# A decode block with attention over a cache and a gated feed-forward: the mask of the PV product pinned in DVE's order, gate and up rows loaded in three pieces, end of attention written ahead of the wd rows

## The chip, the cores and the metric

The kernel runs on one core of one Trainium2 chip. The metric is the device time of one execution in microseconds (us), the median of several runs. The engines of a core work side by side, each through its own list of instructions in order: PE (matrix multiplies; PEld is its weight load), DVE (elementwise work and reductions), ACT (activations), POOL and SP. In this kernel SP issues all large transfers from HBM, one after the other; 16 DMA engines carry them. SBUF is the on-chip memory of 128 partitions, PSUM the accumulators of PE.

## What is computed

One token goes through two branches that are added to it. All data are float32.

```python
def _A_ref(x, k_cache, v_cache, wq, wo):          # x [1,1,576]; caches [1,32,16384,128]
    q = (x @ wq).reshape(B, Sq, H, Dh).transpose(0, 2, 1, 3)
    scores = jnp.einsum("bhqd,bhkd->bhqk", q, k_cache) * (Dh ** -0.5)
    p = _softmax(scores, axis=-1)
    o = jnp.einsum("bhqk,bhkd->bhqd", p, v_cache)
    return o.transpose(0, 2, 1, 3).reshape(B, Sq, H * Dh) @ wo

def _B_ref(x, w_gate, w_up, w_down):              # 576 -> 4608 -> 576
    g = jnp.einsum("bsd,df->bsf", x, w_gate)
    u = jnp.einsum("bsd,df->bsf", x, w_up)
    return jnp.einsum("bsf,fd->bsd", _gelu(g) * u, w_down)

xn = _layernorm(x)
return x + _A_ref(xn, ...) + _B_ref(xn, ...)
```

The two caches hold 32 heads x 16384 positions x 128 numbers each, 537 MB together; the weights add 50 MB. Everything is read once.

## The kernel before

*Memory.* Three large slots of 128 partitions x 64 KiB (`slot()`) hold whatever is being streamed. A slot is handed out again when every reader of its last content has finished; the load into it waits for that on SP, and all later loads wait behind it, as SP issues in order.

*Start.* The first slot (`mix`) takes the remainders of wq, gate and up (`row3`: the fourth row of each partition, `tails`: the last 64 rows), the second wq. `project(steps, ...)` multiplies the normalised token with a weight matrix: one step for each row j of a partition, 12 matmuls a step for gate and up (two passes each in the trace, 24), all accumulating in the same PSUM tile `pg`. `ffn(which)` loads three rows j = 0, 1, 2 of gate (then of up) into a slot with one transfer, runs the steps (row 3, tail, rows 0 to 2), copies the result with ACT into a free part `gc` of the slot (L160), and spreads it by four small POOL transfers over the partitions of `gu`. `ffn_act` makes `hT = gelu(g) * u` of it on DVE; it stands ahead of the first head's work on DVE.

*Heads.* For each of the 32 heads, K and V are loaded into one slot each (8.39 MB per transfer). `qk(h, i)` handles one of eight blocks of 16 keys per partition: DVE multiplies the block in place with the query (L196), then sums ten of the 16 keys (L200), ACT the other six (L199). `softmax(h)` finds the maximum (DVE L204, PE transpose L206, DVE L208, PE L210) and exponentiates on ACT (L214). `pv(h)` multiplies the probabilities with V on PE: 32 matmuls of 4 probability columns x 512 (L220, 64 passes), into `PO[h % 2]`, one of two PSUM tiles. Only a diagonal of each product is wanted: `out_a(h)` masks the tile with `sel` on DVE (L225, "the mask") and sums (L227), `out_b(h)` sums over partitions on PE (L231), and ACT stores the head's column (L232).

*Order.* The framework's scheduler orders the instructions of each engine; it may move an instruction away from its place in the text. `out_a(h - 1)` and `out_b(h - 1)` are written behind block i = 3 of head h. In the built order of this kernel the mask stands right behind `softmax(h - 1)` on DVE, ahead of the first multiply of head h.

*End.* The rows of wd and wo go into the three slots (two and five transfers); wd0 takes a slot that PV of head 30 frees, wd1 and the first 20 rows of wo the slot of the last K, the rest the slot of the last V. PE adds 36 wd rows with `hT` (`add_out`, 144 passes) and 32 wo rows with `oT`, the normalised attention output that comes through a transpose (L286), an ACT copy (L288) and a small transfer. Behind row 26 of wo (`MERGE`) the four partial sums are joined.

Of the kernel before, what the change touches and what calls it, by code (L numbers as in the profile page):

```python
# [13 lines left out]
P = 128  # L14
H, SK, DH = 32, 16384, 128
D, DF = 576, 4608
# [5 lines left out]
DJ = 4  # L22
# [15 lines left out]
def kernel(ctx: ExitStack, tc: tile.TileContext, x, k_cache, v_cache, wq, wo, wg, wu, wd, out):  # L38
    nc = tc.nc
# [12 lines left out]
    wmain = {n: w[:DM].rearrange("(p j) f -> p (j f)", j=DJ) for n, w in (("q", wq), ("g", wg), ("u", wu))}  # L52
# [4 lines left out]
    def slot():  # L57
        return slots.tile([P, R * DH], F32, tag="s", name="slot")

    def load(dst, src):  # L60
        nc.sync.dma_start(dst, src)
        return dst
# [4 lines left out]
    def part_of_mix(src):  # L67
        nonlocal at
        n = src.shape[1]
        at += n  # L70
        return load(mix[:, at - n : at], src)

    ROW3 = 3 * DF
    tails = {"q": part_of_mix(wtail["q"])}
    load(wq_t, wmain["q"])
    row3 = {}
# [15 lines left out]
    sel = cpool.tile([P, 4], F32, name="sel")  # L92
# [28 lines left out]
    def project(steps, group, size):  # L121
        pg = ps_big.tile([P, 3, 512], F32, tag="pb", name="pg")
        for k, (j, rhs) in enumerate(steps):
            for b in range(group // size):
                for q in range(4):
                    lo = q * group + b * size
                    if j < DJ:
                        lhs = xnb[:, j, :]
                    else:
                        lhs = xtb[:, q // 2, :]  # L130
                        lo = (q % 2) * group + b * size
                    nc.tensor.matmul(pg[32 * q : 32 * q + 32, b, :size], lhs, rhs[:, lo : lo + size],  # L132
                                     start=k == 0, stop=k == len(steps) - 1)
        return pg[:, : group // size, :size]

    steps = [(DJ, tails["q"])] + [(j, wq_t[:, j * HD : (j + 1) * HD]) for j in range(DJ)]
# [16 lines left out]
    def ffn(which):  # L153
        n = "gu"[which]
        t = slot()
        w = load(t[:, :ROW3], wmain[n][:, :ROW3])
        gc = t[:, ROW3 : ROW3 + FG]
        steps = [(3, row3[n]), (DJ, tails[n])] + [(j, w[:, j * DF : (j + 1) * DF]) for j in range(3)]
        pg = project(steps, FG, FB)
        nc.scalar.activation(gc.rearrange("p (b f) -> p b f", f=FB), pg, AF.Copy)  # L160
        for q in range(4):
            nc.gpsimd.dma_start(gu[32 * q : 32 * q + 32, which, :], gc[32 * q : 32 * q + 1, :])

    ffn(0)
    ffn(1)

    hT = cpool.tile([P, WD_T], F32, name="hT")
# [54 lines left out]

    def out_a(h):
        o4 = PO[h % 2].rearrange("p (r d) -> p r d", d=DH)
        nc.vector.tensor_mul(o4, o4, sel.unsqueeze(2).to_broadcast([P, 4, DH]))  # L225
        OM[h] = spool.tile([P, DH], F32, name="om")
        nc.vector.tensor_reduce(OM[h], o4.rearrange("p r d -> p d r"), axis=AX.X, op=ALU.add)  # L227

    def out_b(h):
        pc = ps_s.tile([P, 512], F32, tag="sm", name="pc")  # L230
        nc.tensor.matmul(pc[:, :1], OM.pop(h), ones[:, :1], start=True, stop=True)  # L231
        nc.scalar.activation(oall[:, h : h + 1], pc[:, :1], AF.Copy)  # L232

    q_spread(0)
    for h in range(H):
        KT[h] = load(slot(), kv[h])
        VT[h] = load(slot(), vv[h])
        for i in range(NSUB):
            qk(h, i)
            if h == 0 and i == 3:  # L240
                ffn_act()
            if h > 0 and i == 3:
                out_a(h - 1)
                out_b(h - 1)
        KT.pop(h)
        softmax(h)
        if h + 1 < H:
            q_spread(h + 1)
        pv(h)
# [3 lines left out]
    def add_out(pair, lhs, w, last=False):  # L253
        for i in range(2):
            q = 32 * (2 * pair + i)
            nc.tensor.matmul(acc[q : q + 1, :HALF], lhs, w[:, i * HALF : (i + 1) * HALF],  # L256
                             start=q not in seen, stop=last)
            seen.add(q)
# [7 lines left out]
    lo = n0  # L266
# [3 lines left out]
    wd_rows = [wd0[:, j * D : (j + 1) * D] for j in range(a)] + [wd1[:, j * D : (j + 1) * D] for j in range(b)]  # L270
    wo_rows = [wd1[:, (b + j) * D : (b + j + 1) * D] for j in range(n0)]
    wo_rows += [wo1[:, j * D : (j + 1) * D] for j in range(WO_T - n0)]

    out_a(H - 1)
    out_b(H - 1)
    for j, w in enumerate(wd_rows):
        add_out(j % 2, hT[:, j : j + 1], w)

    pl = ps_s.tile([P, 512], F32, tag="sm", name="pl")
    nc.tensor.matmul(pl[:, :H], ones, lsum, start=True, stop=True)  # L280
    rl = cpool.tile([P, H], F32, name="rl")
# [6 lines left out]
    nc.scalar.activation(orow, po[:H, :P], AF.Copy)  # L288
    oT = cpool.tile([P, WO_T], F32, name="oT")
    nc.gpsimd.dma_start(oT, orow)  # L290

    x2 = wo1[:, R * DH - 2 * HALF : R * DH - HALF]
    nc.vector.memset(x2, 0.0)
# [43 lines left out]
```

## Time and profile before

| | |
|---|---|
| time, median of 3 runs | 1481.46 us (1480.93 to 1481.81) |
| the profiled execution | 1480.83 us, its span 1478.9 us |
| busy: DVE / ACT / PE / PEld / POOL | 990.4 / 656.9 / 402.3 / 107.0 / 6.4 us |
| from HBM | 587.6 MB, 397 GB/s over the span |
| TensorE clock granted, mean | 0.626 |

The profile is one execution, recorded by the hardware. Its *groups* give line, engine, operation, output <- input with shapes, count, then busy time, mean ns of one instruction, and the idle time of the engine just ahead of them with what ended it. The *chain that ended last* is followed back from the last instruction, at each step to what released it. *Waits* give who waited for whom: us in total, times, longest. The *timeline* gives start, length, and the instruction. *Windows* give the busy time of each engine in a stretch, the granted clock, the mean busy share of the 16 DMA engines and what they moved; a DMA packet counts where it starts, so that in a short window the rate can be far above or below the real one. L12 is line 12 of the kernel that was profiled.

### The profile page before, as it was taken

The page shows a single profiled execution, that of the slowest core. Times are in us where ns is not written, and L with a number is a line of the kernel's source. Part 1 is how long each engine was busy: PE and PEld are TensorE (multiplying, and loading weights), DVE is VectorE, ACT ScalarE, POOL GpSimd, SP SyncE. Part 2 cuts the span into 40 slices and gives each one's busy share as a digit, 9 for nine tenths or more (in the row PEclk, how much of TensorE's full clock was granted, in tenths as well). Part 3 has the DMA queues.
Part 4 walks back from the last instruction along what each step waited for, and adds up shares of the span by engine and source line. Part 5 has one row for each costly group of instructions (what it writes and reads, how often), then busy time and mean ns, then how long its engine had stood idle before and what let it go on. Part 6 is the DMA issues. An engine that isn't in the chain of part 4 may idle for free.

```text
span 1478.9 us, 10328 instructions
## 1 busy us (share of the span) xinstructions
PE 402.3 (27%) x2881; PEld 107.0 (7%) x2881; DVE 990.4 (67%) x668; ACT 656.9 (44%) x3240; POOL 6.4 (0%) x17
## 2 busy tenths in 40 slices
PE   4413212223222112322321122232211223223118
PEld 1100000000000000000000000000000000000002
DVE  1026787676677887667678876766778776676780
ACT  0014554444445554444455544444455444444550
POOL 0000000000000000000000000000000000000000
PEclk9765555665665566566555656656555665665568
DMA  9999999999899999999989998999999999999897
GB/s 405 426 398 426 422 399 399 415 392 412 371 398 397 397 398 424 399 394 401 396 371 397 424 427 370 398 397 396 399 398 397 425 396 398 386 385 419 373 386 300
DMA packets 11791, 588.31 MB, mean 398 GB/s; under 512 B 1603, under 2 KB 1621, under 8 KB 2006
## 3 DMA queue, kind: packets, MB, share of 16 engines
q1 hardware_dynamic: 11380, 587.60, 93.4%
q8 instruction: 22, 0.36, 0.1%
q14 instruction: 35, 0.29, 0.1%
q0 software_dynamic: 352, 0.06, 0.0%
q10 hardware_dynamic: 2, 0.00, 0.0%
HBM read 587.60 MB, written 0.00 MB: 397 GB/s over the span
## 4 chain that ended last, share of the span: by engine, by line
DVE 55%; PE 24%; ACT 12%; DMA 6%; issue 3%; POOL 0%; ACTq 0%; SPq 0%; DVEq 0%
DVE slot L196 34%; PE po L220 20%; DVE s L200 18%; ACT jk L199 10%; DMA slot<-in_B_w_up_dram 3%; DMA slot<-in_A_wq_dram 2%; DVE po L225 2%; PE acc L256 1%; DMA gu<-slot 1%; PE pg L132 1%; ACT pe L214 1%; PE pb L210 1%; PE pt L206 1%; DVE pm L204 1%; DVE nm L208 1%
## 5 line engine op out<-in xcount | busy, mean ns | idle before, releaser
L199 ACT ACTIVATE jk<-slot 128x128 f32<-128x128 f32 x1536 | 475.3, 309 | 312.5 <-DVE slot L196 268.2
L196 DVE TENSOR_TENSOR slot<-slot,qs 128x2048 f32<-128x2048 f32 x256 | 573.9, 2283 | 0.0
L200 DVE TENSOR_REDUCE s<-slot 128x10 f32<-128x1280 f32 x256 | 367.6, 1478 | 0.0
L220 PE MATMUL po<-slot,pe 128*4 128x512 f32 x2048 | 289.9, 730 | 14.8 <-ACT pe L214 14.5
L199 ACT ACTIVATION_READ_ACCUMULATOR jk<-slot 128x1 f32 x1536 | 286.0, 186 | 0.0
L206 PE MATMUL pt<-ident,pm 128*1 128x128 f32 x32 | 11.9, 372 | 950.0 <-DVE pm L204 950.0
L225 DVE TENSOR_TENSOR po<-po,sel 128x512 f32<-128x512 f32 x32 | 22.4, 700 | 339.8 <-PE po L220 339.8
L232 ACT ACTIVATE oall<-pc 128x1 f32<-128x1 f32 x32 | 5.5, 171 | 349.4 <-PE pc L231 349.4
L206 PEld LDWEIGHTS pt<-ident,pm 128*1 128x1 f32 x32 | 2.5, 79 | 953.3 <-DVE pm L204 901.0
L220 PEld LDWEIGHTS po<-slot,pe 128*4 128x4 f32 x2048 | 54.3, 98 | 229.9 <-issue 205.8
L172 DVE TENSOR_TENSOR t<-gu 128x36 f32<-128x36 f32 x1 | 0.2, 196 | 68.3 <-DMA gu<-slot 68.3
L132 PE MATMUL pg<-slot,xnb 128*32 128x384 f32 (+1 forms) x256 | 29.1, 613 | 36.5 <-DMA slot<-in_B_w_gate_dram 18.7
L212 ACT ACTIVATE nb<-pb 128x1 f32<-128x1 f32 x32 | 5.5, 171 | 57.5 <-PE pb L210 57.5
L231 PE MATMUL pc<-ones,om 128*128 128x1 f32 x64 | 12.2, 260 | 49.8 <-DVE om L227 49.8
L147 PE MATMUL pq<-qrow,ones 1*128 1x128 f32 x64 | 24.8, 488 | 0.0
L227 DVE TENSOR_REDUCE om<-po 128x128 f32<-128x512 f32 x32 | 22.1, 692 | 1.1
L210 PE MATMUL pb<-nm,ones 1*128 1x1 f32 x64 | 17.7, 343 | 14.7 <-DVE nm L208 14.7
L208 DVE TENSOR_REDUCE nm<-pt 1x1 f32<-1x128 f32 x32 | 8.9, 279 | 15.0 <-PE pt L206 15.0
L179 DVE SCALAR_TENSOR_TENSOR hT<-t,gu 128x36 f32<-128x36 f32 x1 | 0.2, 197 | 26.0 <-DMA gu<-slot 26.0
L210 PEld LDWEIGHTS pb<-nm,ones 1*128 1x128 f32 x64 | 15.8, 305 | 23.2 <-issue 22.5
L160 ACT ACTIVATE slot<-pg 128x1152 f32<-128x1152 f32 x2 | 2.3, 1131 | 31.6 <-PE pg L132 31.6
L147 PEld LDWEIGHTS pq<-qrow,ones 1*128 1x128 f32 x64 | 16.0, 307 | 0.6 <-issue 0.6
(61 smaller groups left out, 116.9 us busy)
## 6 DMA issues: line engine op xcount, KB each, us to landing
slot<-in_B_w_down_dram SPq DMA_DIRECT2D x1, 8064.0 KB, 30.7
slot<-in_B_w_gate_dram SPq DMA_DIRECT2D x1, 6912.0 KB, 55.3
slot<-in_B_w_up_dram SPq DMA_DIRECT2D x1, 6912.0 KB
slot<-in_A_wo_dram SPq DMA_DIRECT2D x1, 5760.0 KB, 22.6
slot<-in_B_w_gate_dram SPq DMA_DIRECT2D x1, 2304.0 KB, 28.8
slot<-in_B_w_up_dram SPq DMA_DIRECT2D x1, 2304.0 KB, 37.2
slot<-in_B_w_down_dram SPq DMA_DIRECT2D x1, 2304.0 KB, 7.7
slot<-in_A_wo_dram SPq DMA_DIRECT2D x1, 1728.0 KB, 14.6
```

Of the source, the lines that this page charges most:

```text
L132: nc.tensor.matmul(pg[32 * q : 32 * q + 32, b, :size], lhs, rhs[:, lo : lo + size], start=k == 0, stop=k == len(steps) - 1)
L147: nc.tensor.matmul(pq[:, :DH], ones[r : r + 1, :], qrow[r : r + 1, lo : lo + DH], start=True, stop=True)
L196: nc.vector.tensor_mul(blk, blk, Q[h].to_broadcast([P, SUB, DH]))
L199: nc.scalar.activation(jk, blk[:, n, :], AF.Copy, accum_out=S[h][:, lo + n : lo + n + 1])
L200: nc.vector.tensor_reduce(S[h][:, lo : lo + nv], blk[:, :nv, :], axis=AX.X, op=ALU.add)
L204: nc.vector.reduce_max(pm, S[h], axis=AX.X)
L206: nc.tensor.transpose(pt[:1, :P], pm, ident)
L208: nc.vector.tensor_reduce(nm, pt[:1, :P], axis=AX.X, op=ALU.max, negate=True)
L210: nc.tensor.matmul(pb[:, :1], ones[:1, :], nm, start=True, stop=True)
L220: nc.tensor.matmul(PO[h % 2][q : q + 4, :], pe[:, k : k + 4], vt[:, k * DH : (k + 4) * DH], start=k < 16, stop=k >= R - 16)
L225: nc.vector.tensor_mul(o4, o4, sel.unsqueeze(2).to_broadcast([P, 4, DH]))
L227: nc.vector.tensor_reduce(OM[h], o4.rearrange("p r d -> p d r"), axis=AX.X, op=ALU.add)
```

## The change

Three edits. The gate and the up rows are loaded one row j at a time, so that `project` waits for each alone. The mask is marked so that the scheduler keeps it at its place in the program's text. The block that ends attention (sum of the exponentials, reciprocal, transpose, the transfer of `oT`) is written ahead of the loop over the wd rows.

```diff
     def ffn(which):
         n = "gu"[which]
         t = slot()
-        w = load(t[:, :ROW3], wmain[n][:, :ROW3])
+        steps = [(3, row3[n]), (DJ, tails[n])]
+        for j in range(DJ - 1):
+            lo, hi = j * DF, (j + 1) * DF
+            steps.append((j, load(t[:, lo:hi], wmain[n][:, lo:hi])))
         gc = t[:, ROW3 : ROW3 + FG]
-        steps = [(3, row3[n]), (DJ, tails[n])] + [(j, w[:, j * DF : (j + 1) * DF]) for j in range(3)]
         pg = project(steps, FG, FB)
...
     def out_a(h):
         o4 = PO[h % 2].rearrange("p (r d) -> p r d", d=DH)
-        nc.vector.tensor_mul(o4, o4, sel.unsqueeze(2).to_broadcast([P, 4, DH]))
+        tc.keep_in_program_order(nc.vector.tensor_mul(o4, o4, sel.unsqueeze(2).to_broadcast([P, 4, DH])))
...
     out_a(H - 1)
     out_b(H - 1)
-    for j, w in enumerate(wd_rows):
-        add_out(j % 2, hT[:, j : j + 1], w)
-
     pl = ps_s.tile([P, 512], F32, tag="sm", name="pl")
...
     nc.gpsimd.dma_start(oT, orow)
+
+    for j, w in enumerate(wd_rows):
+        add_out(j % 2, hT[:, j : j + 1], w)
```

In the built order of the changed kernel, DVE has the mask of head h - 1 behind the sum of block four of head h, the sum over it one multiply later, and ACT stores the head's column between its second and third key of block five. SP has four more issues ahead of the first K. The order of the instructions on PE at the end is the same in both kernels.

## The prediction

> **What bounds the kernel now.** I read the page first: the chain that ended last, then the costliest groups.
>
> ```profile
> span 1478.9 us, 10328 instructions
> DVE 55%; PE 24%; ACT 12%; DMA 6%; issue 3%; POOL 0%; ACTq 0%; SPq 0%; DVEq 0%
> L196 DVE TENSOR_TENSOR slot<-slot,qs 128x2048 f32<-128x2048 f32 x256 | 573.9, 2283 | 0.0
> L200 DVE TENSOR_REDUCE s<-slot 128x10 f32<-128x1280 f32 x256 | 367.6, 1478 | 0.0
> L225 DVE TENSOR_TENSOR po<-po,sel 128x512 f32<-128x512 f32 x32 | 22.4, 700 | 339.8 <-PE po L220 339.8
> L227 DVE TENSOR_REDUCE om<-po 128x128 f32<-128x512 f32 x32 | 22.1, 692 | 1.1
> ```
>
> The mask (L225) takes 0.70 us, but DVE stands idle 339.8 us ahead of its 32 instances, 10.6 us a head, waiting for the PV matmuls. The chain in order of time, over one head, shows the loop that this closes:
>
> ```profile
> 598.60 9.88 PE po L220 x64
> 608.50 0.71 DVE po L225
> 609.85 4.48 DVE slot L196 x2
> ...
> 638.57 0.41 ACT jk L199 x2
> 639.00 0.30 DVE pm L204
> ...
> 641.51 8.91 PE po L220 x64
> 650.44 0.71 DVE po L225
> ```
>
> QK of one head (eight multiplies with their sums) fills 609.85 to 638.98, 29.1 us; softmax 2.5 us; PV 8.9 to 9.9 us; mask and the start of its sum 1.4 us; then the next QK. Although the mask is written inside the next head's loop, it runs ahead of that head's first multiply. DVE and PE take turns, and the period is their sum, about 42 us. The loads hang on this loop, as SP's own waits and its issues show:
>
> ```profile
> SPq L61 <- DVE s L200: 954.8, 32, 29.9
> SPq L61 <- PE po L220: 359.2, 32, 12.1
> ...
> 144.88 0.33 SPq L61 DMA_DIRECT2D slot<-in_A_k_cache_dram  x1
> ...
> 608.50 0.33 SPq L61 DMA_DIRECT2D slot<-in_A_k_cache_dram  x1
> 638.99 0.33 SPq L61 DMA_DIRECT2D slot<-in_A_v_cache_dram  x1
> 650.44 0.33 SPq L61 DMA_DIRECT2D slot<-in_A_k_cache_dram  x1
> ...
> 1366.26 0.33 SPq L61 DMA_DIRECT2D slot<-in_A_k_cache_dram  x1
> ```
>
> With three slots, the V load goes out when QK has emptied a K slot (638.99), the K load when PV has emptied a V slot (650.44). From 144.88 to 1366.26 lie 29 periods: 42.1 us each. How far the DMA engines are from being the bound is seen in windows (columns: stretch, length, busy time and count of PE, PEld, DVE, ACT, POOL, granted clock, DMA share, GB/s):
>
> ```profile
> 80.00:174.00 94.00, 13.04 (x95) 3.54 (x87) 58.64 (x37) 39.55 (x192) 1.97 (x4) 0.57 1.00 434
> 637.00:639.90 2.90, 0.37 (x1) 0.08 (x1) 2.12 (x4) 1.84 (x10) 0.00 (x0) 0.50 0.00 0
> ```
>
> While the first heads' transfers stand queued behind each other they flow at 434 GB/s. A K or V transfer is 128 x 16384 x 4 B = 8.389 MB, so 19.33 us, and a pair 38.7 us. In the steady state the queue is dry for about 3 us a head (637 to 639.9: no packet starts): DVE and PE are the bound, but the DMA follows only 3.4 us of 42.1 behind. That limits what can be won.
>
> **The change part by part.** *The pinned mask.* Instruction counts stay. In the changed program's order the mask stands behind the fourth sum of the next head, its sum one multiply later. DVE's turn is then 29.1 + 1.4 (mask and sum, inside QK) + about 1.1 (pm and nm with PE's transpose between, 639.00 to about 640.0) = 31.6 us; PV runs beside the next QK. Below 38.7, so the loads become the bound: the next QK waits for its K. Check that no wait keeps the queue dry: K lands at 0, QK starts about 0.5 later, ends at 31.0 and releases the V load; its first packet comes about 1 us after the issue (638.99, queue dry until 639.9), at 32, while the engines still carry the K transfer until 38.7: 6.7 us to spare. PV ends 2.5 + 9.9 us after QK, at 43.4; the K load that it releases is due at 58. The mask's new wait: QK reaches it at the earliest 1.1 + 4 x 3.6 = 15.5 us after the last QK's end, PV ends 12.4 us after it, so 3 us to spare, and some 10 when QK first waits for K. Behind the mask on DVE stand blocks five to eight, and who waits for those is the V load. ACT's copy of the head's result now stands between the second and third of block five's six sums, where it can wait some 2 us; ACT needs 6 x 0.43 = 2.6 us a block against DVE's 3.6 and catches up. The second PSUM bank of PO covers the mask's late read.
>
> The stage is then priced by bytes: 64 transfers, 536.9 MB, and behind them without a gap wd and wo, 10.62 + 9.44 = 20.05 MB; 556.9 MB at 434 GB/s = **1283 us** from the first K packet to the last weight row.
>
> To this comes what a saturated stream no longer absorbs. Three more windows, and two rows of the page's DMA queues (packets, MB, share):
>
> ```profile
> 1224.30:1224.90 0.60, 0.00 (x0) 0.00 (x0) 0.60 (x2) 0.57 (x4) 0.00 (x0) 0.50 3.84 1638
> 1224.90:1226.20 1.30, 0.00 (x0) 0.00 (x0) 1.30 (x2) 1.21 (x7) 0.00 (x0) 0.50 0.00 0
> 1226.20:1226.40 0.20, 0.00 (x0) 0.00 (x0) 0.20 (x1) 0.17 (x2) 0.00 (x0) 0.50 0.76 328
> ...
> q8 instruction: 22, 0.36, 0.1%
> q14 instruction: 35, 0.29, 0.1%
> ```
>
> In the last round of one transfer, 15 packets (1638 GB/s x 0.6 us = 983 kB, 65.5 kB each) start together, and the sixteenth 1.4 us or more behind: one engine is late. The next dry spell lets it catch up. I put this to instruction blocks (q8: 22 of 16 kB), which one DMA engine has to carry between its packets. Every transfer is split evenly over 16 engines, so without dry spells the lateness of the slowest engine adds up. If all blocks of q8 go through one engine: about 20 of the 22 fall behind the first K, 20 x 1.4 = 28 us. If they spread over all engines, about 2. No row names the engine; I take **28**, because a queue of one sequencer is likelier one ring than sixteen, and keep 2 and 33 (q14 on the same one in part) as ends.
>
> The Trainium skill (Runtime: NRT & Kernel Launch, Instruction fetch mechanics) says that a sequencer fetches its instructions in 16 KiB blocks over a DMA queue of its own and that this is mostly hidden; q8's 0.36 MB in 22 packets agrees with the size, and by "hidden" the term would be about 0.
>
> *Gate and up rows in three transfers.* Four more issues on SP, ahead of K0's issue, which waits anyway. Startup rows:
>
> ```profile
> 24.40:30.00 5.60, 5.08 (x24) 1.18 (x28) 0.00 (x0) 0.00 (x0) 0.00 (x0) 1.00 1.01 431
> 72.00:77.00 5.00, 2.57 (x36) 0.85 (x32) 0.34 (x2) 0.00 (x0) 0.00 (x0) 1.00 0.07 18
> ...
> 59.24 8.80 PE L132 MATMUL pg<-slot,xnb 128*32 128x384 f32 x72 [18.71 <-DMA slot<-in_B_w_gate_dram]
> 69.31 2.14 PE L132 MATMUL pg<-slot,xnb 128*32 128x384 f32 x24 [1.26 <-ACT slot L160]
> 76.71 0.33 SPq L61 DMA_DIRECT2D slot<-in_A_k_cache_dram  x1
> 103.73 0.20 DVE L179 SCALAR_TENSOR_TENSOR hT<-t,gu 128x36 f32<-128x36 f32 x1 [25.97 <-DMA gu<-slot]
> ```
>
> PE now starts on the gate at 59.24, when all three rows are in, and needs 8.80 us; with thirds only the last 24 passes are left, 2.1 us warm to 3.9 cold (72 passes: the first half at twice the price). The chain gate, ACT copy, spread to gu, K0's issue (76.71) moves 4.9 to 6.7 us ahead, to 70 to 72, before the up rows are in; the queue's dry spell (18 GB/s in 72 to 77) closes. K0's first packet comes at about 73.7 instead of 77.7: **4 us won** (0 to 4.7). The thirds are of the size of the row of 24.4 to 30, which ran at 431 GB/s, so splitting costs 0.2 us on 14 MB. QK of head 0 waits for hT, whose spread of up goes out some 4 us sooner: V1's load at about 129 instead of 133, just ahead of K1's end at 131.7.
>
> By the Trainium skill (SBUF — State Buffer, The DMA setup-cost knee) each transfer pays about 2 us, so four more would be 8 us and the total 1402; but the stretch at 434 GB/s above has five transfers in it and no such cost, as each is queued while the one ahead flows.
>
> *End of attention ahead of the wd rows.* Nothing: it is so already.
>
> ```profile
> 1454.28 0.39 PE L286 MATMUL pot<-ident,on 128*32 128x128 f32 x1 [0.75 <-DVE on L284]
> 1454.60 10.35 PE L256 MATMUL acc<-slot,hT 128*1 128x288 f32 x144
> ...
> 1472.34 3.08 PE L256 MATMUL acc<-slot,oT 128*1 128x288 f32 x24
> 1475.94 0.62 SPq L308 DMA_DIRECT2D out_dram<-slot  x1
> ...
> 1468.00:1470.00 2.00, 2.00 (x40) 0.78 (x36) 0.00 (x0) 0.00 (x0) 0.00 (x0) 1.00 0.17 61
> ```
>
> The transpose (L286) runs before the first wd row, and PE's order at the end is the same in the changed program. What changes is who waits: now the last bytes come just under 1470, while PE works without a break from 1454.6 and ends at 1475.4. In the changed kernel V31 lands about 49 us (20.05 MB and 2 late blocks) before the last row, PV ends 24 us after it, PE is through the wd rows at +39 and waits for rows. Behind the last landing remain the final 24 passes (3.08), the add (0.45) and the output (1475.94 to the end, 3.0): **6.6 us** (5 to 9).
>
> **The sum.** 73.7 + 1283 + 28 + 6.6 = 1391 us of span (now 1478.9). The profiled run took 1480.83, 1.9 more than its span, and stands 0.6 under the median of the runs: 1391 + 2.5 = **1394 us**, 5.9% less. Of the 88 us won, about 78 come from the steady state (42.1 to 39.5 a head), 4 from the start, the rest from the end.
>
> **The rivals.** *A, the forecast (0.64):* DMA-bound, one engine late: 1394; with its own ends (lateness 22 to 33, start, tail) 1385 to 1403.
> *B, lateness does not add up (0.20):* blocks spread over engines: 28 becomes 2, 1368. For it: no row names the engine. Against: single late engines recur.
> *C, overlap costs something (0.11):* no row shows a DVE multiply beside a PV matmul, as they take turns now. If PE's reading of the V slot slows DVE, the first 6.7 us a head are free; each further one costs some 31 us. Between 6.7 and 9.5 lost: 1394 to 1480, mostly near the low end, since ACT reads the same slot as DVE today and the multiply keeps 2.28 us.
> *D, slower (0.05):* the same place, taken to its end: DVE and PE exclude each other while PV runs. Then QK takes 31.0 + 9.9 = 40.9, the V load's packets start at 41.9, 3.2 late, and the restart costs a little more: some 42.6 a head against 42.1, +15 us, less 9 at start and end: 1487. From about 9.5 us lost a head it is no gain. Against it: nothing in the rows makes DVE stop for PE.
> The Trainium skill (SBUF — State Buffer, A bandwidth-pool intuition that's wrong) holds that PE, ACT and DMA have ports of their own, so C and D would cost nothing; no run here shows it yet.
> *That the mask stays where it was* is excluded by the order of the changed program; that the third edit does nothing is in the sum.
>
> **How the numbers follow.** A and B lie within 1366 to 1403. The range takes in B's value, A's ends and the lower half of C: 1365 to 1425; outside lie D, C's upper part and some of B's lower side, under 0.15. Faster by over 0.2% (about what a measurement here can tell from no change): A, B and nearly all of C, 0.95; within 0.2%: 0.01; slower: 0.04.
>
> **What would show it.** DVE idle ahead of the mask near 0 in place of 339.8; DVE's idle time now ahead of the first multiply, put to the K load, some 6 to 7 us a head; K issues 39.5 us apart (38.7 under B, over 40 under C); DMA near 98% of the span at about 423 GB/s; multiplies still 2.28 us (under C and D longer beside PV); K0's issue near 71; the last bytes about 6.6 us before the end. The forecast is wrong if multiplies stretch, if the V issue comes later than 37 us after a K landing, or if the period is 38.7.

## The result, and the profile after

| | before | changed kernel |
|---|---|---|
| time, median | 1481.63 us (1480.93 to 1483.29) | 1392.28 us (1390.13 to 1394.2, 4 runs) |
| ratio | | 0.9395 (0.9378 to 0.9412) |
| the profiled execution, and its span | 1480.83, 1478.9 us | 1390.13, 1388.4 us |

The changed kernel is 6.0% faster; forecast were 1394 us. Its line numbers are two higher than before: L198 is the multiply, L202 the sum on DVE, L201 the sums on ACT, L227 the mask, L222 the PV product. The page of the changed kernel, its busy times, DMA queues (packets, MB, share), the chain that ended last and the costliest groups:

```profile
span 1388.4 us, 10333 instructions
PE 415.1 (30%) x2881; PEld 113.9 (8%) x2881; DVE 990.0 (71%) x668; ACT 653.6 (47%) x3240; POOL 6.3 (0%) x17
q1 hardware_dynamic: 11956, 587.60, 98.9%
q14 instruction: 35, 0.29, 0.1%
HBM read 587.60 MB, written 0.00 MB: 423 GB/s over the span
DMA 49%; DVE 34%; PE 13%; ACT 4%; issue 1%; SPq 0%; POOL 0%; DVEq 0%; ACTq 0%
L198 DVE TENSOR_TENSOR slot<-slot,qs 128x2048 f32<-128x2048 f32 x256 | 576.4, 2283 | 211.2 <-DMA slot<-in_A_k_cache_dram 211.2
L227 DVE TENSOR_TENSOR po<-po,sel 128x512 f32<-128x512 f32 x32 | 22.0, 688 | 11.3 <-PE po L222 11.3
```

DVE's work is what it was (990.0 against 990.4 us, the multiply still 2283 ns). The 339.8 us of idle time ahead of the mask are down to 11.3, and those belong to one wait, the last head's, behind which no other head's multiplies stand. DVE's idle time is now ahead of the first multiply of a head, 211.2 us in 31 heads, and K ends it. The DMA has gone from 6% to 49% of the chain. One head in the timeline (start, length, instruction; in brackets the idle time before it and what ended it), DVE's rows and SP's issues:

```profile
606.20 4.49 DVE L198 TENSOR_TENSOR slot<-slot,qs 128x2048 f32<-128x2048 f32 x2 [7.03 <-DMA slot<-in_A_k_cache_dram]
...
617.80 2.87 DVE L202 TENSOR_REDUCE s<-slot 128x10 f32<-128x1280 f32 x2
620.59 0.69 DVE L227 TENSOR_TENSOR po<-po,sel 128x512 f32<-128x512 f32 x1
621.18 2.28 DVE L198 TENSOR_TENSOR slot<-slot,qs 128x2048 f32<-128x2048 f32 x1
...
634.88 1.49 DVE L202 TENSOR_REDUCE s<-slot 128x10 f32<-128x1280 f32 x1
637.54 0.29 DVE L206 TENSOR_REDUCE pm<-s 128x1 f32<-128x128 f32 x1 [1.18 <-ACT jk L201]
645.77 4.49 DVE L198 TENSOR_TENSOR slot<-slot,qs 128x2048 f32<-128x2048 f32 x2 [7.19 <-DMA slot<-in_A_k_cache_dram]
```

```profile
144.52 0.33 SPq L61 DMA_DIRECT2D slot<-in_A_k_cache_dram  x1
...
609.53 0.33 SPq L61 DMA_DIRECT2D slot<-in_A_k_cache_dram  x1
637.53 0.33 SPq L61 DMA_DIRECT2D slot<-in_A_v_cache_dram  x1
649.72 0.33 SPq L61 DMA_DIRECT2D slot<-in_A_k_cache_dram  x1
...
1278.99 0.33 SPq L61 DMA_DIRECT2D slot<-in_A_k_cache_dram  x1
```

The mask stands at 620.59 with no wait ahead of it, 14.4 us behind the start of QK, and the multiply behind it follows at once. QK fills 606.20 to 637.5, 31.3 us, and DVE then stands for 7.2 us until the next K is in. From 144.52 to 1278.99 lie 29 periods of 39.1 us (42.1 before).

### The profile page after: what moved, and what is told of

Its sections match the earlier page's. It is cut to its first block, busy times and chain, and to the rows that moved or that the text cites. A ratio compares the mean times of both kernels' runs of the same rounds, so it can differ in the third digit from the quotient of the medians.

```text
span 1388.4 us, 10333 instructions
## 1 busy us (share of the span) xinstructions
PE 415.1 (30%) x2881; PEld 113.9 (8%) x2881; DVE 990.0 (71%) x668; ACT 653.6 (47%) x3240; POOL 6.3 (0%) x17
## 3 DMA queue, kind: packets, MB, share of 16 engines
q1 hardware_dynamic: 11956, 587.60, 98.9%
## 4 chain that ended last, share of the span: by engine, by line
DMA 49%; DVE 34%; PE 13%; ACT 4%; issue 1%; SPq 0%; POOL 0%; DVEq 0%; ACTq 0%
DMA slot<-in_A_k_cache_dram 41%; DVE slot L198 20%; DVE s L202 11%; PE po L222 10%; DMA slot<-in_B_w_up_dram 3%; ACT jk L201 3%; DMA slot<-in_A_wo_dram 2%; DMA slot<-in_A_wq_dram 2%; DMA gu<-slot 1%; PE pg L132 1%; DVE po L227 1%; DVE om L229 1%; PE acc L258 1%; ACT pe L216 1%; PE pt L208 0%
## 5 line engine op out<-in xcount | busy, mean ns | idle before, releaser
L201 ACT ACTIVATE jk<-slot 128x128 f32<-128x128 f32 x1536 | 475.0, 309 | 552.1 <-DVE slot L198 509.7
L198 DVE TENSOR_TENSOR slot<-slot,qs 128x2048 f32<-128x2048 f32 x256 | 576.4, 2283 | 211.2 <-DMA slot<-in_A_k_cache_dram 211.2
L202 DVE TENSOR_REDUCE s<-slot 128x10 f32<-128x1280 f32 x256 | 370.2, 1477 | 1.1
L222 PE MATMUL po<-slot,pe 128*4 128x512 f32 x2048 | 294.0, 738 | 14.8 <-ACT pe L216 14.5
L201 ACT ACTIVATION_READ_ACCUMULATOR jk<-slot 128x1 f32 x1536 | 286.4, 186 | 0.0
L233 PE MATMUL pc<-ones,om 128*128 128x1 f32 x64 | 18.6, 359 | 438.2 <-DVE om L229 438.2
L222 PEld LDWEIGHTS po<-slot,pe 128*4 128x4 f32 x2048 | 54.5, 98 | 233.8 <-issue 209.7
L233 PEld LDWEIGHTS pc<-ones,om 128*128 128x128 f32 x64 | 15.8, 308 | 467.9 <-DVE om L229 467.9
L206 DVE TENSOR_REDUCE pm<-s 128x1 f32<-128x128 f32 x32 | 9.1, 286 | 36.7 <-ACT jk L201 36.7
L227 DVE TENSOR_TENSOR po<-po,sel 128x512 f32<-128x512 f32 x32 | 22.0, 688 | 11.3 <-PE po L222 11.3
```

The costliest lines, as they stand in the source:

```text
L198: nc.vector.tensor_mul(blk, blk, Q[h].to_broadcast([P, SUB, DH]))
L201: nc.scalar.activation(jk, blk[:, n, :], AF.Copy, accum_out=S[h][:, lo + n : lo + n + 1])
L202: nc.vector.tensor_reduce(S[h][:, lo : lo + nv], blk[:, :nv, :], axis=AX.X, op=ALU.add)
L222: nc.tensor.matmul(PO[h % 2][q : q + 4, :], pe[:, k : k + 4], vt[:, k * DH : (k + 4) * DH], start=k < 16, stop=k >= R - 16)
L227: tc.keep_in_program_order(nc.vector.tensor_mul(o4, o4, sel.unsqueeze(2).to_broadcast([P, 4, DH])))
```

## The experiments

By its size the forecast was right, so the runs were spent on its terms: what the pin gives and what the other two edits give together, which engine's instruction blocks make one DMA engine late, and whether the rest of what separates the kernel from its bytes can be had. Four theories are named in the expectations. *P*: PE's instruction blocks (queue q8) all go through one DMA engine, as the prediction took it. *A*: it is ACT's blocks (q14) instead. *L*: the V load goes out too late to follow K without a break, so that DVE's turn still counts. *N*: the time above the bytes has nothing to do with instruction blocks. The kernel before took between 1480.43 and 1481.05 us (medians) beside all these runs.

**The changed kernel once more, unaltered.**

> The changed kernel again, on the chip of the next three, as their measure: 1392 us (1390 to 1395) under every theory.

1393.31 us (1392.08 to 1393.87), ratio 0.9406 (0.9393 to 0.9419). This is the base of the differences below.

**More blocks for PE.** Twenty one-element products a head, behind `out_b`:

```diff
                 out_b(h - 1)
+                pad = ps_s.tile([P, 512], F32, tag="sm", name="pad")
+                for n in range(20):
+                    tc.keep_in_program_order(nc.tensor.matmul(pad[:1, n : n + 1], ones[:1, :1], ones[:1, :1], start=True, stop=True))
```

> 20 one-element matmuls a head, behind the head's last sum on PE, where PE is idle for over 10 us; their result is used nowhere. They add 31 x 20 x 2 passes x 2 instructions = 2480 instructions of 64 B, some 10 blocks of 16 kB, to PE's instruction queue q8 (23 packets now), and nothing else that waits. Theory P (the prediction's: all of q8 is carried by one DMA engine, 1.4 us of lateness a block): +14 us, about 1406. Theory A (ACT's blocks in q14 go through one engine, PE's are spread over the engines): +1 us, 1391 to 1394. Theory N (the time above the bytes has nothing to do with instruction blocks): +0.

**More blocks for ACT.** Thirty-two one-element copies a head, behind the spread of the next query:

```diff
             q_spread(h + 1)
+            for _ in range(32):
+                pad = spool.tile([1, 1], F32, name="pad", bufs=1)
+                tc.keep_in_program_order(nc.scalar.activation(pad, ones[:1, :1], AF.Copy))
```

> 32 one-element copies a head on ACT, behind the spread of the query, where ACT waits some 7 us for the next K; their result is used nowhere. They add 31 x 32 = 992 instructions of 64 B, some 8 blocks of 8 kB, to q14 (35 packets in the execution now). Theory A: each block makes one DMA engine about 0.65 us later (its own 0.31 and the slower packet beside it), +5 us, about 1397; q14 has 43 packets. Theory P: q8 unchanged, +0. Theory N: +0.

The instruction queues on the page of the kernel with more products, and under it of the one with more copies:

```profile
q8 instruction: 32, 0.52, 0.1%
q14 instruction: 35, 0.29, 0.0%
```

```profile
q8 instruction: 23, 0.38, 0.1%
q14 instruction: 42, 0.34, 0.1%
```

Ten more blocks of q8 cost nothing: 1391.93 us (1390.55 to 1392.62), 1.4 less than the base. Theory P falls. Seven more of q14 cost 7.1 us: 1400.39 (1396.21 to 1402.67). The copies themselves are 7.4 us a head, beside DVE's wait for K, as one head of that kernel shows:

```profile
603.36 0.33 SPq L61 DMA_DIRECT2D slot<-in_A_v_cache_dram  x1
...
605.89 7.42 ACT L253 ACTIVATE pad<-ones 1x1 f32<-1x1 f32 x32
612.25 4.50 DVE L198 TENSOR_TENSOR slot<-slot,qs 128x2048 f32<-128x2048 f32 x2 [7.85 <-ACT pad L253]
```

The bracket puts DVE's wait down to the copies, but the multiply starts at 612.25, before the last of them ends (613.31): they did not hold it in this head. Nor in another: by the records of the landings, the first multiply of every head but the first starts at most 0.5 us behind the last landing of its K, and the next V load goes out 31.3 us behind that start, as in the changed kernel. Theory N falls with this run. Seven blocks at the 0.69 us that is worked out below are 4.8 us; where the rest of the 7.1 comes from is open, and the four runs spread over 6.5 us.

**Fewer blocks for ACT.** The reverse: ACT sums fewer of the 16 keys of a block, DVE more.

```diff
-N_ACT = 6
+N_ACT = 2
```

> N_ACT 2 in place of 6: ACT sums two of 16 keys, DVE 14. The output is the same. 1024 sums fewer on ACT are 2048 instructions, 16 blocks of 8 kB fewer in q14 (35 to about 19). DVE's sum over 14 keys takes about 2.0 us in place of 1.48, QK about 33 in place of 29, so the V load still goes out some 36 us behind the K landing, in time for a stream of 38.7 a head. Theory A: 16 x 0.65 = 10 us less, about 1382. Theory P and N: 1392, or more if DVE's longer turn starts to bind.

> N_ACT 4: ACT sums four of 16 keys, DVE 12; same output. 1024 instructions fewer on ACT, 8 blocks fewer in q14 (35 to 27). Theory A alone (one late engine, 0.69 us a block of q14): 8 x 0.69 = 5.5 us less, about 1387.5. Theory A with a price for a V load that goes out late (theory L): its issue moves from 31.3 to about 32.9 us behind QK's start, still over 3 us ahead of the need, so the same 1387 to 1389. Neither (the two-key variant's 1391 was all that fewer blocks can give): 1391 to 1392.

> N_ACT 3: 12 blocks of q14 fewer than in the changed kernel (35 to 23), the V load's issue about 33.4 us behind QK's start (31.3 there, 32.3 with four keys, 34.5 with two). Theory A alone: 12 x 0.69 = 8.3 us less than 1393, about 1385. Theory A with L (below some 3 us of lead of the V load over the first engine that runs dry, all first packets of the transfer are slow): still 1385 to 1387, since the lead is about 1 us longer than with two keys. If L bites at this lead already: 1389 to 1391.

| N_ACT | time, us | blocks of q14 | V issue ahead of the next QK's start, one head |
|---|---|---|---|
| 6 (base) | 1393.31 (1392.08 to 1393.87) | 35 | 8.0 us |
| 4 | 1387.44 (1385.58 to 1389.01) | 27 | 7.0 us |
| 3 | 1383.48 (1382.44 to 1384.0) | 23 | 5.9 us |
| 2 | 1391.18 (1389.88 to 1392.1) | 19 | 4.4 us |

From 6 to 4 and 3 the time falls by 5.9 us for 8 blocks and 9.8 for 12, 0.7 to 0.8 us a block, as theory A wants. At 2 the fall is given back. The head of the kernel with N_ACT = 2, DVE's rows and SP's issue:

```profile
641.83 2.02 DVE L202 TENSOR_REDUCE s<-slot 128x14 f32<-128x1792 f32 x1
...
643.95 0.33 SPq L61 DMA_DIRECT2D slot<-in_A_v_cache_dram  x1
...
648.33 4.50 DVE L198 TENSOR_TENSOR slot<-slot,qs 128x2048 f32<-128x2048 f32 x2 [3.35 <-DMA slot<-in_A_k_cache_dram]
```

DVE still waits 3.35 us for K, so by DVE's own turn nothing should be lost. But the V load goes out at 643.95, and by the records of the single packets the first DMA engine is through with K at 645.43, 1.5 us later. Of the 16 first packets of that V, 15 then take 2.5 to 4.2 us instead of 2.42.

**A late load in the changed kernel.** To test L by itself, DVE sums block six of each head four times:

```diff
-        nc.vector.tensor_reduce(S[h][:, lo : lo + nv], blk[:, :nv, :], axis=AX.X, op=ALU.add)
+        for _ in range(4 if i == 5 else 1):
+            nc.vector.tensor_reduce(S[h][:, lo : lo + nv], blk[:, :nv, :], axis=AX.X, op=ALU.add)
```

> One of the sums of each head is done four times on DVE in place of once, with the same output: DVE's turn grows by 4.3 us, the V load's issue from 31.3 to about 34.5 us behind QK's start, where it was with two keys on ACT; ACT's instructions are as in the changed kernel, q14 at 35 or 36. Theory A alone (only the one late engine sets the pace, and it has work until 38.7): 1392 to 1394. Theory L (a V load issued 2 us ahead of its need starts with slow packets, and this is what took the gain of the two-key variant): +5 to +9, 1397 to 1401.

1394.82 us (1394.12 to 1395.13), 1.5 over the base: between the two expectations, so this run doesn't decide. Its V issues lie some 5 us ahead of the next QK's start, not 8.

**The mask pinned alone.** The kernel before with the second edit only:

```diff
-        nc.vector.tensor_mul(o4, o4, sel.unsqueeze(2).to_broadcast([P, 4, DH]))
+        tc.keep_in_program_order(nc.vector.tensor_mul(o4, o4, sel.unsqueeze(2).to_broadcast([P, 4, DH])))
```

> The kernel before with the pinned mask alone. By the prediction's sum the pin is worth all but the 4 us of the start: 1392 + 4 = 1396 us. By the trace of the changed kernel, whose first K lands only 1 us sooner than before (last engine at 97.4 in place of 98.4): 1393 to 1394. The third edit adds nothing under both.

**All but the pin.** The changed kernel with that line as it was before:

> The changed kernel without the pin: gate and up in thirds, end of attention ahead. By the prediction: the DVE and PE loop stays at 42.1 us a head, the start gives 4 us: 1477. By the trace of the changed kernel, where head 0's QK starts 0.7 us sooner (103.15 in place of 103.87): 1480 to 1481, no change.

The mask pinned alone: 1395.89 us (1395.84 to 1396.83), 85 below the kernel before; the changed kernel is 2.6 (base) to 3.6 us (first comparison) faster still. All but the pin: 1476.6 (1475.97 to 1478.82), ratio 0.9976 (0.9965 to 0.9986), 4.5 us below the kernel before. So the pin gives 85 us, and the other two edits together 3 to 4.5. In the kernel without the pin the mask's line has its wait back:

```profile
L227 DVE TENSOR_TENSOR po<-po,sel 128x512 f32<-128x512 f32 x32 | 22.4, 699 | 339.2 <-PE po L222 339.2
```

**Fewer instructions for the same work.** Blocks of 32 keys, of which ACT sums four (then six); the mask stays in the middle of the head:

```diff
-SUB = 16
+SUB = 32
...
-N_ACT = 6
+N_ACT = 4
...
-            if h == 0 and i == 3:
+            if h == 0 and i == 1:
                 ffn_act()
-            if h > 0 and i == 3:
+            if h > 0 and i == 1:
                 out_a(h - 1)
```

> Blocks of 32 keys in place of 16, ACT sums four of them (two of 16 in proportion, as in the variant with two keys), the mask behind the second of four blocks, same output. q14 as there, 19 or fewer. DVE's turn loses the start of eight instructions, the V load's issue comes at about 33.9 in place of 34.5. Theory A alone: 16 x 0.69 = 11 less than 1393, 1382. Theory A with L: part of it, 1383 to 1388. If the two-key variant's missing gain has to do with the number of ACT's instructions and not with the V load's lead: 1391.

> Blocks of 32 keys, ACT sums six of them (three of 16 in proportion), same output. q14 about 23 or fewer, the V load's issue at about 32.8 us. Theory A: 1385, with L the same, as the lead is that of the variant with four of 16 keys, which won what A said.

With four keys 1381.71 us (1379.51 to 1382.91), the best of all kernels here, 0.8% below the changed kernel; with six 1382.53 (1380.84 to 1384.0), no difference. q14 is down to 16 and 20 blocks. Against the base that is 11.6 us for 19 blocks, 0.6 each. By theory A the four blocks between the two kernels should be worth 2.8 us; 0.8 were measured, less than either's spread.

**The same with the V load 0.9 us later.** One more sum over six keys in each head, nothing else changed against the best kernel:

```diff
         nc.vector.tensor_reduce(S[h][:, lo : lo + nv], blk[:, :nv, :], axis=AX.X, op=ALU.add)
+        if i == 2:
+            nc.vector.tensor_reduce(S[h][:, lo : lo + 6], blk[:, :6, :], axis=AX.X, op=ALU.add)
```

> The variant with blocks of 32 keys and four of them on ACT, with one more sum on DVE over six keys, once a head (its result is already there, the output the same): some 0.9 us more of DVE, the V load's issue at 34.9 us behind QK's start in place of 34.0, 0.4 later than in the variant with two keys (34.5). q14 stays at 16 or 17. Theory A alone: 1382, as before, since DVE still waits some 3 us a head for its K. Theory L (with no single late engine all sixteen reach the end of a K transfer together, and a V load that comes less than some 2 us ahead gives all of them slow first packets): back to 1390 or above.

1391.87 us (1388.57 to 1399.69): 10 us lost by the medians, with the same 16 blocks of q14. One head of the best kernel (first the V issue, then the next QK; DVE's wait for K in all, number of waits, longest), and below it of the kernel with the extra sum:

```profile
639.86 0.33 SPq L61 DMA_DIRECT2D slot<-in_A_v_cache_dram  x1
...
644.99 8.76 DVE L198 TENSOR_TENSOR slot<-slot,qs 128x4096 f32<-128x4096 f32 x2 [4.09 <-DMA slot<-in_A_k_cache_dram]
...
DVE slot L198 <- DMA slot<-in_A_k_cache_dram: 117.3, 30, 5.1
```

```profile
638.61 0.94 DVE L204 TENSOR_REDUCE s<-slot 128x6 f32<-128x768 f32 x1
...
643.44 0.33 SPq L61 DMA_DIRECT2D slot<-in_A_v_cache_dram  x1
...
647.44 8.76 DVE L198 TENSOR_TENSOR slot<-slot,qs 128x4096 f32<-128x4096 f32 x2 [2.96 <-DMA slot<-in_A_k_cache_dram]
...
DVE slot L198 <- DMA slot<-in_A_k_cache_dram: 101.5, 30, 4.5
```

DVE has 3.4 us to spare in each of 30 heads (101.5 / 30), yet 0.94 us of work in it costs 10 us over 32 heads: what was used up is not DVE's time but the lead of the V load, 5.1 us ahead of the next QK in the one kernel, 4.0 in the other (5.0 and 4.5 on the mean of the heads). Theory L holds here, beside A: A alone had nothing to lose in this run.

## Why the prediction was right, point by point

*The mask and its wait.* Right, as all rows it named show: the mask no longer waits, it comes more than 10 us behind the start of QK (14.4), the loads set the period, and DMA fills 98.9% of the span at 423 GB/s. The pin alone explains 85 of the 89 us. V's issue comes 31.3 us behind the start of QK (31.0 forecast behind the landing). The period is 39.1 (39.5).

*The bytes.* Right. By the packet records, from the last engine's end of K0 (97.36) to that of the last V (1334.64) lie 1237.3 us for 63 transfers; 63 x 19.33 is 1217.8, the remaining 19.5 are the lateness. Between the two profiled executions the span fell by 90.5 us: 1.0 of them up to K0's end (98.4 before), 83.8 in this stretch, 5.7 behind it. Forecast were 4, 78 and the rest: the steady state gave more than its share, as the lateness is smaller.

*The lateness, 28 us.* Its mechanism was right (one DMA engine carries blocks between its packets, and in a full stream that adds up), its size some 8 us too large, and its source wrong: not PE's q8 but q14. The price of a q8 block was read rightly: the engine that is late in the prediction's windows at 1224 us had carried one at 1192.83 (0.93 us, and the packet behind it 2.92). But in the packet records of the changed kernel between 130 and 560 us, nine of the eleven q14 blocks stand in the row of one engine, which has no gap, while the seven of q8 lie in seven different engines. A q14 block takes 0.31 us there, and the packet beside it 2.80 instead of 2.42: 0.69 us a block. From K0's end to V31's end there are 34 blocks; nine elevenths of them, 28, would be 19 us. The step that failed is the sentence "a queue of one sequencer is likelier one ring than sixteen": for q8 it is not so. That the sum came out near is luck: 20 blocks of q8 at 1.4 us give nothing here, and about 28 of q14 at 0.69 stand in their place. The run with ten more q8 blocks and those with more and fewer q14 blocks show which queue it is. Rival B (nothing adds up, 1368) fell with 19.5 us measured. The Trainium skill (Runtime: NRT & Kernel Launch, Instruction fetch mechanics) says that crossing from one block to the next is mostly hidden. The runs agree for PE's blocks (ten more, -1.4 us), and not for q14's, some 19 us or 1.4% of the time.

*The start, 4 us.* Right in sum (3 to 4.5 us, with the third edit), with two steps off. Rows of the changed kernel's timeline, and the window that ran at 18 GB/s before:

```profile
61.77 1.13 ACT L162 ACTIVATE slot<-pg 128x1152 f32<-128x1152 f32 x1 [20.78 <-PE pg L132]
63.20 2.12 POOL L164 DMA_DIRECT2D gu<-slot  x4 [61.90 <-ACT slot L162]
73.47 0.20 DVE L174 TENSOR_TENSOR t<-gu 128x36 f32<-128x36 f32 x1 [65.14 <-DMA gu<-slot]
73.62 0.33 SPq L61 DMA_DIRECT2D slot<-in_A_k_cache_dram  x1
...
72.00:77.00 5.00, 1.61 (x20) 0.46 (x16) 0.77 (x4) 0.23 (x1) 0.00 (x0) 0.82 0.99 381
```

The copy of gate came early enough, but its spread landed 10.3 us behind its issue (63.20 to 73.47), as its packets stand among those of the up rows, and K0 was issued at 73.62, not at 70 to 72. That is 3.1 us ahead of the kernel before (76.71) and came while the last up rows were still flowing: the dry spell closed (381 GB/s), and K0's first packet started at 74.6 us by the packet records (73.7 forecast, 77.7 before). The other step is the spread of up, forecast 4 us sooner: V1's load, which waits for QK of head 0, went out at 132.30 (129 forecast, 133.02 before), in the second execution of the same kernel at 130.10.

*The end.* Nothing had been forecast for the third edit; PE's order is the same, and the run with the pin alone, 1395.9, came out as expected (1396), with nothing for the third edit. That edit was not run by itself. The chain's last stretch, in the timeline of the changed kernel:

```profile
1362.71 10.22 PE L258 MATMUL acc<-slot,hT 128*1 128x288 f32 x144
1374.40 6.49 PE L258 MATMUL acc<-slot,oT 128*1 128x288 f32 x104 [1.47 <-DMA slot<-in_A_wo_dram]
1381.96 3.08 PE L258 MATMUL acc<-slot,oT 128*1 128x288 f32 x24
1385.56 0.63 SPq L310 DMA_DIRECT2D out_dram<-slot  x1
```

PE waits for the rows, as forecast, and the last 24 passes begin as the last row lands (1382.04 by the packet records): 6.4 us to the end of the span (6.6).

*Rivals C and D (overlap costs).* Both fell: PV runs beside the start of QK now, and the multiply took 2283 ns in both kernels; the first one of a head, which lies beside PV, took 2292 (2282 before). The Trainium skill (SBUF — State Buffer, A bandwidth-pool intuition that's wrong) says that readers of SBUF do not share one bandwidth, and that slowing comes from structural stalls such as a port lock. The trace agrees: 10 ns more beside PV.

*What the prediction did not see.* "First packet about 1 us after the issue" is not all that a late load costs. In two of the experiments a V load that went out 4 to 5 us ahead of the next QK cost about 10 us, with DVE still idle. The changed kernel has such slow first packets, too. In the head shown above, V is issued at 637.53, the first engine is through with K at 639.28, and 11 of the 16 first packets take 2.5 to 4.1 us. But there the engine that carries q14's blocks is so late that it hides them: by the records of the landings its K is in 2.8 us behind that of the fifteenth engine (mean of heads 2 to 31). With N_ACT = 2 the last engine is 0.6 us behind the fifteenth, in the last run 0.5, so that there what the slow packets cost the others can set the pace. This reading fits the run with the fourfold sum (0.6 us behind, q14's lateness as before, 1.5 us lost), but no run separates the two. Open is the exact point: the mean lead of the V load on the next QK is 5.0 us in the best kernel, 4.8 with N_ACT = 2, 4.5 in the last run. Which instructions besides ACT's q14 carries wasn't tried either.

## What to carry to other kernels

Where two engines take turns through one consumer of the other's result, put that consumer in the middle of the next turn's work, and first check how far the next resource is behind: here the DMA followed 3.4 us of 42.1 later, and that was what could be won. Once the transfers set the pace, count the instructions of each engine, too: larger blocks for the same sums were worth 0.8%. And judge a load by its lead on the end of the transfer ahead, engine by engine, not by whether its consumer still has idle time.

## What the runs showed of the hardware

- q14's blocks, 8 kB each, go mostly through one DMA engine (nine of eleven between 130 and 560 us) and delay it by about 0.7 us each; q8's, 16 kB, fall on different engines (seven of seven) and cost nothing that can be measured (10 more: -1.4 us).
- A 64 KiB packet takes 2.42 us in the flow. With the next load issued 1.5 us ahead of the first engine's end, 15 of 16 first packets took 2.5 to 4.2 us. Over 140 to 1270 us, 338 packets of this size took more than 2.55 us in the kernel with N_ACT = 2, 143 in the best one, 307 in the one with the extra sum, 304 in the changed kernel. The windows of that stretch, first with N_ACT = 2, then of the best kernel, end in 428 and 431 GB/s:

```profile
140.00:1270.00 1130.00, 319.58 (x2042) 83.45 (x2034) 1009.00 (x577) 214.67 (x1065) 0.00 (x0) 0.61 1.00 428
```

```profile
140.00:1270.00 1130.00, 318.86 (x2075) 84.19 (x2071) 998.94 (x349) 212.66 (x1073) 0.00 (x0) 0.62 1.00 431
```
